# Storing the last two token tiles by half tiles, one request for both row groups

## The chip, the cores and the metric

The kernel runs on one core of a Trainium2 chip. The metric is the device time of one execution in microseconds. Before the change the median of three runs is 279.37 us (279.22 to 279.82). The profiled execution spans 277.0 us. TensorE's granted clock is full over the whole span.

## The reference

A linear attention with cosine weights feeds a dense layer with a gated activation. With B = 8, H = 8, S = 576, D = 64, d_model = 512 and d_ff = 2048:

```python
q_p, k_p = phi(q, c, s), phi(k, c, s)        # relu(x)*cos and relu(x)*sin, concatenated
kv  = einsum('bhsf,bhsd->bhfd', k_p, v)
num = einsum('bhsf,bhfd->bhsd', q_p, kv)
den = einsum('bhsf,bhf->bhs', q_p, k_p.sum(axis=2)) + 1e-6
x   = (num / den).transpose(0, 2, 1, 3).reshape(4608, 512)
h   = x @ w_in                               # 4608 x 2048
out = (h / (1 + exp(-beta * h))) @ w_out     # 4608 x 512, float32
```

The 4608 token rows are worked on in nine chunks of 512 rows. A chunk has four tiles of 128 rows. Only the last matmul of the last chunk, and the way its result leaves for DRAM, is touched by the change.

## The kernel before

The product with `w_out` is done for a pair of token tiles at once, in seven block products instead of eight (`"1"` to `"7"`), with sums of the operands prepared ahead and sums of the results made while they leave PSUM. `o1` and `o2` are the two 128 x 512 output tiles of the pair in SBUF. Each is written in two halves of 256 columns (HM = 256, DM = 512):

```python
def c4():
    h = HM // 2 if last else HM
    nc.scalar.copy(o2[:, 0:h], b_ps[:, 0:h])
    if last:
        nc.vector.tensor_copy(o2[:, h:HM], b_ps[:, h:HM])
        store(c, pr + 2, o2, 0, HM)

def stored(key, op):
    def do():
        op()
        waits[key[0]].discard(key[1:])
        if not waits[key[0]] and not (last and key[0] == "2"):
            store(c, pr + (2 if key[0] == "2" else 0), o2 if key[0] == "2" else o1)
        if last and key == "2a7":
            store(c, pr + 2, o2, HM, DM)
    return do

waits = {"1": {"a2", "a3"}, "2": {"a7", "c4"}}
# ...
"c4": stored("2c4", c4),
"a2": stored("1a2", lambda: nc.vector.tensor_tensor(o1[:, 0:HM], a_ps, p1, **add)),
"a3": stored("1a3", lambda: nc.vector.tensor_tensor(o1[:, HM:DM], e_ps, u, **add)),
"a7": stored("2a7", lambda: nc.vector.tensor_tensor(o2[:, HM:DM], b_ps, p5, **add)),
```

`last` is true for the second pair of the last chunk, which the list of operations calls `y`; the first pair of that chunk is `x`. The list ends, with the operations that only prepare later chunks left out:

```
ox5 ox4 c4x o7y oy3 o2y o3y oy4 c4y
```

So on VectorE the sums of the last pair come in the order a7 (right half of `o2`), a2 (left half of `o1`), a3 (right half of `o1`), and c4 (left half of `o2`) is last of all. In this text they are called a7y, a2y, a3y and c4y.

The rows of a tile lie in DRAM in two groups. Partition p of the first 64 is row 9p + n of a batch of 576 rows, and partition p of the second 64 is row 9p + n + 1. A store sends one request for each group:

```python
out_v = out.rearrange("(b p n) m -> b n p m", b=B, n=NQ)

def store(c, tt, o_sb, m0=0, m1=DM):
    for hf in range(2):
        bb, n = divmod((c * TCH + tt * P) // HP + hf, NQ)
        eng = nc.gpsimd if c < 7 else (nc.sync, nc.scalar)[hf] if c == NTC - 1 and tt % 2 else nc.sync
        eng.dma_start(out=out_v[bb, n][:, m0:m1], in_=o_sb[hf * HP : (hf + 1) * HP, m0:m1])
```

In the last chunk the tiles 0 and 2 (pair `x`) go to SyncE's queue with both groups; the tiles 1 and 3 (pair `y`) go with the first group to SyncE's queue and with the second to ScalarE's.

Of the kernel before, what the change touches and what calls it, by code (L numbers as in the profile page):

```python
# [16 lines left out]
P = 128  # L17
NQ = 9
# [4 lines left out]
def kernel(  # L23
# [14 lines left out]
    nc = tc.nc  # L38

    B, H, S, D = q.shape  # L40
    DM = H * D
# [3 lines left out]
    TCH = 512  # L45
    NTC = B * S // TCH
    TT = TCH // P
    NB = TCH // 64
    HP = P // 2
# [35 lines left out]
    HM = DM // 2  # L85
# [417 lines left out]

    out_v = out.rearrange("(b p n) m -> b n p m", b=B, n=NQ)

    def store(c, tt, o_sb, m0=0, m1=DM):
        for hf in range(2):
            bb, n = divmod((c * TCH + tt * P) // HP + hf, NQ)
            eng = nc.gpsimd if c < 7 else (nc.sync, nc.scalar)[hf] if c == NTC - 1 and tt % 2 else nc.sync
            eng.dma_start(out=out_v[bb, n][:, m0:m1], in_=o_sb[hf * HP : (hf + 1) * HP, m0:m1])  # L510

    def o_mm(c, tt, jts, cols=1):
        o_ps = ps[:, (2, 3, 0, 1)[tt] if c == 0 else 2 + tt // 2]
        for jt in jts:
            w = DM // cols if jt > 0 else DM
            for m0 in range(0, DM, w):
                nc.tensor.matmul(o_ps[:, m0 : m0 + w], lhsT=gs[c, jt // 4][:, jt % 4, tt * P : (tt + 1) * P],  # L517
                                 rhs=wout[:, jt, m0 : m0 + w],
                                 start=(jt == 0), stop=(jt == JT - 1 and m0 == DM - w))
        if jts[-1] < JT - 1:  # L520
            return
        o_sb = osb_pool.tile([P, DM], FP32, name="o_sb", tag="o_sb")
        nc.scalar.copy(o_sb, o_ps)
        store(c, tt, o_sb)
# [7 lines left out]
    def late(c):  # L532
        made[c] = made.get(c, 0) + 1
        return made[c] > 14 - SPLITS.get(c, (0, 0))[1]

    def o_fast(c, pr, banks):

        b_ps, e_ps, a_ps = (ps[:, k_, 0:HM] for k_ in banks)
        tok = slice(pr * P, (pr + 1) * P)
        last = c == NTC - 1 and pr == 1  # L540

        def prod(dst, left, right, start, stop, pieces=False):
            order = (0, 1, 2, 3, 4, 5, 7, 6) if c + 1 >= B else range(JT // 2)
            for i in order:
                w = HM // 2 if i and pieces else HM
                for m in range(0, HM, w):
                    nc.tensor.matmul(dst[:, m : m + w], lhsT=left(i), rhs=right[:, i, m : m + w],  # L547
                                     start=start and i == 0,
                                     stop=stop and i == order[-1], skip_group_check=True)

        def g_part(r, hf):
            def at(i):
                jt = 2 * i + r
                return gs[c, jt // 4][:, jt % 4, hf * (TCH // 2) + pr * P : hf * (TCH // 2) + (pr + 1) * P]
            return at

        def s_part(t):
            return lambda i: t[:, i, tok]

        o1 = osb_pool.tile([P, DM], FP32, name="o_sb", tag="o_sb")  # L560
        o2 = osb_pool.tile([P, DM], FP32, name="o_sb", tag="o_sb")
        p1 = part.tile([P, HM], FP32, name="p1", tag="p1")
        p5 = part.tile([P, HM], FP32, name="p5", tag="p5")
        u = part.tile([P, HM], FP32, name="u", tag="u")

        def c4():
            h = HM // 2 if last else HM
            nc.scalar.copy(o2[:, 0:h], b_ps[:, 0:h])
            if last:
                nc.vector.tensor_copy(o2[:, h:HM], b_ps[:, h:HM])  # L570
                store(c, pr + 2, o2, 0, HM)

        def stored(key, op):
            def do():
                op()
                waits[key[0]].discard(key[1:])
                if not waits[key[0]] and not (last and key[0] == "2"):
                    store(c, pr + (2 if key[0] == "2" else 0), o2 if key[0] == "2" else o1)
                if last and key == "2a7":
                    store(c, pr + 2, o2, HM, DM)  # L580
            return do

        waits = {"1": {"a2", "a3"}, "2": {"a7", "c4"}}
        add = dict(op=ALU.add)
        return {
            "1": lambda: prod(b_ps, g_part(0, 0), B11, True, False, late(c)),
            "5": lambda: prod(e_ps, s_part(S1), T1, True, False, late(c)),
            "6": lambda: prod(b_ps, s_part(S2), T2, False, False, late(c)),
            "2": lambda: prod(a_ps, g_part(1, 0), B21, True, True, late(c)),
            "7": lambda: prod(b_ps, s_part(S3), T3, False, False, late(c)),  # L590
            "3": lambda: prod(e_ps, s_part(S4), B22, False, True, late(c)),
            "4": lambda: prod(b_ps, g_part(1, 1), T4, False, True, late(c)),
            "c1": lambda: nc.scalar.copy(p1, b_ps),
            "c5": lambda: nc.scalar.copy(p5, e_ps),
            "cu": lambda: nc.scalar.copy(u, b_ps),
# [5 lines that stand above are left out]
# [463 lines left out]
```

## Time and profile before

| what | before |
|---|---|
| median of 3 runs | 279.37 us |
| span of the profiled execution | 277.0 us |
| TensorE busy | 269.3 us |
| last matmul starts | 272.44 us |
| last copy out of PSUM ends (VectorE, L570) | 273.57 us |
| last store request starts (SyncE) | 273.97 us |
| stores requested from 268.9 us on | 10 requests, 1.05 MB |

Times within the execution count from the start of the span. The page of a profile gives busy times of each engine, the span in 40 slices, the DMA queues, the chain of work that ended last, and groups of instructions by source line. DMA q1 is the queue of SyncE and q10 the queue of ScalarE; SPq and ACTq are the instruction queues of these two engines, in which a store is one instruction of about half a microsecond. "To landing" is the time from the start of that instruction to the last of the store's completion signals. A share of DMA time is a share of all 16 DMA engines. L510 is the store, L547 the block products, L568 and L570 the two halves of c4, and L597, L598 and L599 are a2, a3 and a7.

### The profile page before, as it was taken

Reading aid. Unit: us, or ns where it says so; the run is one execution under the profiler, and the core shown is the slowest. Engines: PE = TensorE matmul, PEld = TensorE weight load, DVE = VectorE, ACT = ScalarE, POOL = GpSimd, SP = SyncE. Lnnn points to the kernel's source line nnn. Section 1 sums busy time; section 2 is a strip of 40 time slices with the busy share of each in tenths; the row PEclk is TensorE's granted clock in tenths of the full one; section 3 lists DMA queues with packets and bytes.
Section 4 is the critical chain, followed back from the end, with each engine's and each line's share of the span. In section 5 each row is a group of like instructions: output and inputs, shape, how many; then the busy total and the mean of one; then the engine's idle time right before and its main releaser. Section 6 shows DMA issues by size and latency. Waiting matters only on the chain.

```text
span 277.0 us, 8756 instructions
## 1 busy us (share of the span) xinstructions
PE 269.3 (97%) x3615; PEld 193.5 (70%) x3621; DVE 209.0 (75%) x548; ACT 179.9 (65%) x357; POOL 69.8 (25%) x89
## 2 busy tenths in 40 slices
PE   8889999999999999999999999999999999999993
PEld 8454455446875587549854898788768886888783
DVE  5889977696979885358659995798679779559832
ACT  5778857793236667675767586896685179429811
POOL 1444000606281085006420632016400140000000
PEclk9999999999999999999999999999999999999999
DMA  7999999999998999992898289715400640024006
GB/s 250 373 395 380 394 388 307 373 199 393 213 231 298 280 222 265 381 135 43 211 374 216 49 220 273 130 22 107 114 2 12 116 114 4 0 59 96 2 2 149
DMA packets 50584, 53.98 MB, mean 195 GB/s; under 512 B 31201, under 2 KB 31473, under 8 KB 50545
## 3 DMA queue, kind: packets, MB, share of 16 engines
q1 hardware_dynamic: 47584, 45.82, 58.8%
q0 software_dynamic: 2688, 7.34, 9.6%
q8 instruction: 28, 0.46, 0.7%
q10 hardware_dynamic: 272, 0.27, 0.4%
q14 instruction: 12, 0.09, 0.2%
HBM read 36.71 MB, written 9.44 MB: 167 GB/s over the span
## 4 chain that ended last, share of the span: by engine, by line
PE 91%; DMA 3%; DVE 2%; SPq 1%; issue 1%; ACTq 0%; ACT 0%
PE ps L547 33%; PE ps L380 25%; PE ps L468 11%; PE ps L517 8%; PE ps L422 7%; PE ps L293 4%; DMA raw_v<-in_v_dram 3%; PE ps L272 3%; DVE xs L315 1%; SPq L79 1%; PE ps L352 0%; DVE win L115 0%; PE ps L234 0%; DVE rden L308 0%; DVE vb L209 0%
## 5 line engine op out<-in xcount | busy, mean ns | idle before, releaser
L380 PE MATMUL ps<-xt,win 128*128 128x512 bf16 (+1 forms) x327 | 71.1, 375 | 0.1
L388 ACT ACTIVATE g_t<-ps,beta 128x512 bf16<-128x512 f32 x80 | 54.4, 689 | 17.6 <-PE ps L380 16.7
L380 PEld LDWEIGHTS <-win 128*128 128x128 bf16 x327 | 31.4, 98 | 35.2 <-issue 0.4
L547 PEld LDWEIGHTS <-S 128*128 128x128 bf16 x508 | 47.4, 98 | 5.1
L510 POOL DMA_DIRECT2D out_dram<-o_sb x56 | 30.8, 556 | 72.3 <-DVE o_sb L598 32.7
L413 ACT ACTIVATE g_t<-ps,beta 128x512 bf16<-128x512 f32 x64 | 41.2, 696 | 3.4 <-PE ps L422 2.2
L547 PEld LDWEIGHTS <-g_t 128*128 128x128 bf16 x388 | 35.4, 98 | 3.9
L399 DVE TENSOR_TENSOR S<-g_t 128x512 bf16<-128x512 bf16 (+1 forms) x70 | 24.3, 382 | 10.4 <-ACT g_t L388 8.2
L547 PE MATMUL ps<-wout,g_t 128*128 128x256 bf16 (+1 forms) x254 | 30.2, 267 | 0.0
L547 PE MATMUL ps<-wout,S 128*128 128x256 bf16 (+1 forms) x254 | 29.3, 267 | 0.0
L222 POOL TENSOR_TENSOR qs<-qt,tanr 128x1152 bf16<-128x1152 bf16 x8 | 18.9, 2378 | 40.2 <-DVE S L399 17.2
L547 PE MATMUL ps<-T,S 128*128 128x256 bf16 (+1 forms) x254 | 29.0, 267 | 0.0
L217 ACT ACTIVATE vb<-raw_v,sin 128x256 bf16<-128x256 f32 (+1 forms) x57 | 25.5, 502 | 0.5 <-DMA raw_v<-in_v_dram 0.5
L422 PE MATMUL ps<-xt,win 128*128 128x512 bf16 (+1 forms) x111 | 24.0, 350 | 0.0
L315 DVE TENSOR_TENSOR xs<-ps,rden 128x768 bf16<-128x768 f32 (+4 forms) x26 | 22.8, 884 | 0.8
L517 PE MATMUL ps<-wout,g_t 128*128 128x512 bf16 (+1 forms) x117 | 21.6, 330 | 0.4 <-issue 0.2
L219 DVE TENSOR_SCALAR vb<-raw_v,cos 128x256 bf16<-128x256 f32 x63 | 20.5, 383 | 0.0
L468 PE MATMUL ps<-w_stage 128*128 128x256 bf16 x120 | 20.3, 273 | 0.0
L468 PEld LDWEIGHTS <-w_stage 128*128 128x128 bf16 x160 | 15.5, 98 | 3.9
L517 PEld LDWEIGHTS <-g_t 128*128 128x128 bf16 x123 | 11.6, 98 | 7.7
L222 POOL TENSOR_TENSOR w_stage<-qt,tanr 128x1152 bf16<-128x1152 bf16 x4 | 9.5, 2380 | 28.4 <-DVE den L304 15.1
L547 PE MATMUL ps<-T,g_t 128*128 128x256 bf16 (+1 forms) x134 | 15.6, 261 | 0.0
(104 smaller groups left out, 380.4 us busy)
## 6 DMA issues: line engine op xcount, KB each, us to landing
raw_v<-in_v_dram SPq DMA_DIRECT2D x7, 1152.0 KB, 11.0
raw_k<-in_k_dram SPq DMA_DIRECT2D x7, 1152.0 KB, 9.2
raw_q<-in_q_dram SPq DMA_DIRECT2D x7, 1152.0 KB, 8.2
out_dram<-o_sb POOLq DMA_DIRECT2D x56, 128.0 KB, 4.3
w_stage<-in_moe_w_in_dram SPq DMA_DIRECT2D x3, 1024.0 KB, 13.2
w_stage<-in_moe_w_out_dram SPq DMA_DIRECT2D x2, 1024.0 KB, 7.6
w_stage<-in_moe_w_out_dram SPq DMA_DIRECT2D x4, 512.0 KB, 12.2
out_dram<-o_sb SPq DMA_DIRECT2D x13, 128.0 KB, 2.4
```

Of the source, the lines that this page charges most:

```text
L217: nc.scalar.activation(o, a, AF.Copy, scale=t[:, n : n + 1])
L222: return eng.tensor_tensor(dst.rearrange("q n (g p) -> q n g p", g=2), src.rearrange("q n (g p) -> q n g p", g=2), tanr[:, n0:n1].unsqueez ...
L315: nc.vector.tensor_tensor(o.rearrange("q j n s d -> q j (n s) d"), nv[:, :, a:z, :, 0:D].rearrange("q j n s d -> q j (n s) d"), rden[:, :, ...
L380: nc.tensor.matmul(ps[:, h_bank(c, jt), i * 64 : (i + w) * 64], lhsT=win[jt // 4][:, mi, (jt % 4) * P : (jt % 4 + 1) * P], rhs=xt[:, i : i ...
L388: nc.scalar.activation(gs[c, jt // 4][:, jt % 4], ps[:, h_bank(c, jt)], AF.Silu, scale=beta[:, jt : jt + 1])
L399: return nc.vector.tensor_tensor(o, l, r, op=op)
L413: nc.scalar.activation(gs[c, jt // 4][:, jt % 4], ps[:, bank], AF.Silu, scale=beta[:, jt : jt + 1])
L422: nc.tensor.matmul(ps[:, bank, o * 64 : z * 64], lhsT=win[jt // 4][:, mi, (jt % 4) * P : (jt % 4 + 1) * P], rhs=xt[:, o:z, jp, g * HP : (g ...
L468: nc.tensor.matmul(dst, lhsT=left[:, g], rhs=right[:, :, g * HP : (g + 1) * HP], start=start and g == 0, stop=stop and g == 1, skip_group_ ...
L510: eng.dma_start(out=out_v[bb, n][:, m0:m1], in_=o_sb[hf * HP : (hf + 1) * HP, m0:m1])
L517: nc.tensor.matmul(o_ps[:, m0 : m0 + w], lhsT=gs[c, jt // 4][:, jt % 4, tt * P : (tt + 1) * P], rhs=wout[:, jt, m0 : m0 + w], start=(jt == ...
L547: nc.tensor.matmul(dst[:, m : m + w], lhsT=left(i), rhs=right[:, i, m : m + w], start=start and i == 0, stop=stop and i == order[-1], skip ...
```

## The change

Three things change, all in the last pair of the last chunk. The second row group and the first now go out with one request, for each half tile that a sum of VectorE ends (a7y, a2y, a3y): a7y and a2y on ScalarE's queue, a3y on SyncE's. The tile `o1` is no longer stored whole after its second half; each half is stored when it is summed. And c4y is copied by ScalarE alone, in one copy of 256 columns, where ScalarE and VectorE copied 128 columns each; its store stays as it was, two requests of 64 rows. The aim is to let each half leave as early as it can, with fewer requests in front of the last one, and to have no hand-over between two engines in the last copy.

```diff
+    def store_both(tt, o_sb, m0, m1, eng):
+        bb, n = divmod(((NTC - 1) * TCH + tt * P) // HP, NQ)
+        eng.dma_start(out=out_v[bb, n : n + 2, :, m0:m1], in_=o_sb[:, m0:m1])
+
     def store(c, tt, o_sb, m0=0, m1=DM):
 ...
         def c4():
-            h = HM // 2 if last else HM
-            nc.scalar.copy(o2[:, 0:h], b_ps[:, 0:h])
+            nc.scalar.copy(o2[:, 0:HM], b_ps)
             if last:
-                nc.vector.tensor_copy(o2[:, h:HM], b_ps[:, h:HM])
                 store(c, pr + 2, o2, 0, HM)
 
         def stored(key, op):
             def do():
                 op()
                 waits[key[0]].discard(key[1:])
-                if not waits[key[0]] and not (last and key[0] == "2"):
+                if last:
+                    if key[1] == "a":
+                        tile_, m0 = (o2, HM) if key == "2a7" else (o1, HM if key == "1a3" else 0)
+                        store_both(pr + (2 if key == "2a7" else 0), tile_, m0, m0 + HM,
+                                   nc.sync if key == "1a3" else nc.scalar)
+                elif not waits[key[0]]:
                     store(c, pr + (2 if key[0] == "2" else 0), o2 if key[0] == "2" else o1)
-                if last and key == "2a7":
-                    store(c, pr + 2, o2, HM, DM)
             return do
```

In the program as built, nothing else differs. TensorE and GpSimd have the same instructions with the same waits. VectorE has one copy less. In the last pair SyncE has two requests (a3y, c4y) where it had three, and ScalarE still has three (a7y, a2y, c4y). A `store_both` request has the pattern [2 rows apart by 512][64 rows apart by 4608][256 columns] on its DRAM side, counted in elements, and [128 partitions][256 columns] on its SBUF side. A `store` request has [64][256 or 512] on both sides.

## The prediction

> **What bounds the kernel now.** I read the page first: the line of busy times and the engine shares of the chain that ended last.
>
> ```profile
> span 277.0 us, 8756 instructions
> ...
> PE 269.3 (97%) x3615; PEld 193.5 (70%) x3621; DVE 209.0 (75%) x548; ACT 179.9 (65%) x357; POOL 69.8 (25%) x89
> ...
> PE 91%; DMA 3%; DVE 2%; SPq 1%; issue 1%; ACTq 0%; ACT 0%
> ```
>
> TensorE is busy 97% of the span and is 91% of the chain. The change touches none of its instructions, so everything up to the last matmul should stay where it is. What can move is what follows: the last matmul starts at 272.44 and the span ends at 277.0, so some 4.3 us are at stake on the good side, 1.5% of the time. On the bad side there is no such limit.
>
> Second, the chain of waits in the window 266 to 277 (start, length, what).
>
> ```profile
> 265.95 5.91 PE ps L547 x54
> ...
> 271.88 0.44 DVE o_sb L598
> ...
> 272.34 0.47 ACTq L510
> ...
> 272.98 0.27 ACT o_sb L568
> ...
> 273.28 0.29 DVE o_sb L570
> ```
>
> The reader should see that the chain leaves TensorE at a3y (L598) and goes through ScalarE's request for the tile that a3y completes (0.47 us in ScalarE's queue), before ScalarE's part of c4y may start at 272.98. VectorE's part waits for ScalarE's (273.28) and ends at 273.57. TensorE's last completion signal in the trace is at 272.73, and the other copies of this line start 0.02 us after theirs, so c4y is about 0.23 us late behind that request.
>
> Third, the timeline of the two queues in the window 268.5 to 278, and the DMA issues in the window 266 to 277 (requests, KB each, median us to landing).
>
> ```profile
> 268.91 5.61 SPq L510 DMA_DIRECT2D out_dram<-o_sb  x7
> ...
> 271.01 1.80 ACTq L510 DMA_DIRECT2D out_dram<-o_sb  x2
> ...
> 273.60 0.47 ACTq L510 DMA_DIRECT2D out_dram<-o_sb  x1
> ```
>
> ```profile
> out_dram<-o_sb SPq DMA_DIRECT2D x5, 128.0 KB, 2.4
> out_dram<-o_sb ACTq DMA_DIRECT2D x2, 64.0 KB, 2.2
> out_dram<-o_sb ACTq DMA_DIRECT2D x1, 128.0 KB, 2.7
> out_dram<-o_sb SPq DMA_DIRECT2D x2, 64.0 KB, 2.4
> ```
>
> Narrower windows give the seven starts of SyncE: 268.91, 269.43, 271.40, 271.92, 272.61, 273.25, 273.97. From 271.40 on it is a queue without a gap: a3y's data are there at 272.31 and its first row group is asked for at 273.25; c4y's are there at 273.57 and are asked for at 273.97. That last request lands 2.1 us later, at 276.07, and 0.93 us of closing barriers follow.
>
> Fourth, the table of stretches (columns: us, busy and count of PE, PEld, DVE, ACT, POOL; then clock, DMA share, GB/s).
>
> ```profile
> 272.00:274.00 2.00, 0.72 (x7) 0.39 (x4) 0.60 (x2) 0.27 (x1) 0.00 (x0) 1.00 0.79 182
> 274.00:275.00 1.00, 0.00 (x0) 0.00 (x0) 0.00 (x0) 0.00 (x0) 0.00 (x0) 1.00 1.03 254
> 275.00:276.00 1.00, 0.00 (x0) 0.00 (x0) 0.00 (x0) 0.00 (x0) 0.00 (x0) 1.00 0.59 168
> ```
>
> The second number from the right is what matters: from 272 to 275 all sixteen DMA engines are nearly full. The tail of this kernel is moved by sixteen engines together, and there is little slack if a part of them drops out.
>
> **What the Trainium skill says.** "DMA: Bandwidth & Descriptors", section "Why a DMA increments its semaphore by 16 and not by 1", says how many engines carry a request from SyncE or ScalarE: take the slowest dimension that is not 1 on each side, and the number is the largest k up to 16 that divides both; and the k engines are the lowest-numbered ones. Its section "Rules for kernel authors" warns that an outermost dimension below 16 confines the whole request to that many engines. The trace before agrees as far as it can: every store has 64 on both sides, and in the window 275.1 to 276 ScalarE's last request shows as 80 packets, which is 64 rows and 16 completion writes, one for each engine. No request of the kernel before has a small outermost dimension, so its trace doesn't test the rule for small k. The same page, section "Queues, rings and completion order", says that the queues of SyncE and ScalarE run on the same sixteen engines, each in its own order. Also this agrees: in 274 to 275 packets of both queues make the share of 1.03 together.
>
> **The change, part by part.**
>
> *The copy.* It removes ScalarE's request of 0.47 us between a3y and c4y, as a2y's request now follows a2y (ready at 271.30) and should be issued by about 272.1. The copy can start at 272.73 + 0.02 = 272.75, takes 0.37 (the row of L568 with 256 columns in the timeline), and ends at 273.13 instead of 273.57: 0.44 us earlier. VectorE's 0.29 us copy and the hand-over go.
>
> *The queue of SyncE.* It has one request less. 271.40, 271.92, then a3y at 272.61 (0.55 long), then c4y at about 273.25 instead of 273.97: 0.72 us earlier. ScalarE's own c4y request comes at 273.16 instead of 273.60. Were that all, the last landing would be at 273.25 + 2.1 = 275.35 and the time 279.37 - 0.7 = 278.65 us.
>
> *The new requests.* Here is the step that decides. A `store_both` request has 2 as its outermost dimension in DRAM and 128 in SBUF; the largest k that divides both is 2. By the page each of the three requests is carried by two engines, and all three by the same two, in place of sixteen. Each of the two then writes 64 rows of 1 KB for each request, 192 in all.
>
> What a 1 KB row costs an engine comes from two answers of the trace, each "packets, MB, share of 16 engines":
>
> ```profile
> q10 hardware_dynamic: 80, 0.07, 22.4%
> q1 hardware_dynamic: 444, 0.88, 100.2%
> ```
>
> The first is the window 275.1 to 276: 0.224 x 16 x 0.9 us = 3.23 us for 64 rows of 1 KB and 16 completions, hence at most 50 ns a row. The second is a window of long loads, 23.5 to 26: 1.002 x 16 x 2.5 us = 40.1 us for 0.88 MB, hence 22 bytes per ns for an engine, and 1 KB = 47 ns, in a stream without pauses. I take 47 ns.
>
> The work of one of the two engines, from its first packet on: three requests, 192 x 0.047 = 9.0 us. Its share of the two whole-group stores of pair `x` (4 rows of 2 KB each): by the window 270 to 270.5, 48 packets took 0.874 x 16 x 0.5 = 7.0 us, 146 ns each, so 8 x 0.146 = 1.2 us. Its share of c4y: 8 x 0.047 = 0.4 us. The sum is 10.6 us. The first packet of a7y appears some 1.2 us after its request at 271.01, at 272.2. The engine is done at 272.2 + 10.6 = 282.8. The completion follows the last packet by about 0.35 us in the trace before (last packets at 275.7, landing at 276.07): 283.15. With the 0.93 us of barriers the span is 284.1, which is 7.1 us more. Were the `x` rows as quick as loads (8 x 0.09) it would be 0.5 us less. I put it at +6.8: 279.37 + 6.8 = **286.2 us**, a ratio of 1.024.
>
> The gains above don't subtract. c4y's rows are appended to rings of the two slow engines, so an earlier copy only waits longer; and a tail of 7 us hides every change of tenths.
>
> **Rivals.**
>
> *The requests spread over sixteen engines after all.* For it: the DRAM side holds 128 rows of equal length, and a generator that counted rows could spread them; the trace before shows no request with a 2 outside. Against it: the page states the rule for exactly this case and says that k = 2 was seen. It would give 278.6 us, 0.3% faster, and the DMA share of the tail would stay near 1 for three microseconds. I give it about 15%.
>
> *The rings fill and ScalarE is stuck.* Two requests on ScalarE's queue put 2 x 65 entries on each of two rings. In the trace before, requests that normally take 0.47 us took 1.4 to 2.8 us in the long loads (at 10.1 and 26.7 to 32.5), where some 115 or more packets per engine were outstanding. So ScalarE may be held in the a2y request by up to 1.5 us and copy c4y late. It would cost nothing as long as the two engines still have work, which they have until about 282. It adds to the time only if the ring runs empty between two requests: up to 1.5 us more, 287.7.
>
> *A row costs more in a long row of writes.* Loads show 47 ns, the last stores of 1 KB up to 50. Stores from 64 partitions with 2 KB rows show 146 ns with all engines at work; half of that for 1 KB is 73 ns and would add 192 x 0.026 = 5 us: 291. With fourteen engines idle I expect less competition, not more, but this keeps the upper side long.
>
> *The two engines share the rows otherwise, or pause at completions.* A few tenths either way.
>
> **Range and chances.** Two engines: 85%. Within that case the lowest sum I can build is 0.046 x 192 + 8 x 0.09 + 0.4 = 9.9 us of work, +6.4 us, 285.8; I allow 2 us below for packets that overlap more than the shares show, and 3.3 above for stalls and slower rows. Range 283.8 to 289.5. The 2% line lies at 284.96, near the low side of this case, so about nine tenths of it is slower by over 2%: 0.77. The rest of it and the sixteen-engine case are within 2%: 0.22. Faster by over 2% would need more than the 4.3 us after the last matmul: 0.01.
>
> **What the changed profile would show.** If I am right: the matmuls end at the same time; c4y's copy is one row of 0.37 us starting near 272.75 or up to 1.5 us later; from 275 to 282 the DMA share is near 2/16 = 0.125 with 40 to 45 GB/s and no engine busy; the three new requests (a7y, a2y, a3y) need about 5, 10 and 9 us to land instead of 2 to 3, as a7y has the engines nearly to itself at first and the other two then share them; and each shows 128 rows with 2 completion packets. If the share of the tail stays above 0.5 and the requests land in 2 to 3 us, the step on k is wrong and so is the prediction. If the share is 0.125 but the tail ends much later, it is the 47 ns. If TensorE's end has moved, I have misjudged the part that I called untouched.

## The result, and the profile after

The median goes from 279.56 us (four runs of the kernel before) to 288.33 us (287.97 to 289.73), a ratio of 1.0324 with a 95% interval of 1.0286 to 1.0362. The kernel after is 3.2% slower. The ratio is taken over all the runs; the quotient of the two medians is 1.0314. The profiled span is 285.8 us where it was 277.0.

The first lines of the page after (span, then busy time, share and instructions of each engine):

```profile
span 285.8 us, 8759 instructions
...
PE 268.5 (94%) x3621; PEld 192.1 (67%) x3621; DVE 208.3 (73%) x547; ACT 180.0 (63%) x357; POOL 69.4 (24%) x89
```

TensorE's busy time is the same within 1 us (it was 269.3), in a span that is 8.8 us longer. All engines have only lost share. The time was added where none of them works. In the trace, TensorE's last completion signal stands at 272.76, and at 272.73 before.

The chain of waits in the window 266 to 286 (start, length, what):

```profile
271.91 0.43 DVE o_sb L603
...
272.35 0.45 ACTq L508
...
272.97 0.37 ACT o_sb L571
```

In this kernel L508 is the new request for both row groups, called the joint request from here on, L514 the plain store, L571 the copy and L603 is a3. The last copy is now one piece of 0.37 us, but it starts at 272.97, no earlier than before: it still stands behind a request in ScalarE's queue, now that of a2y (L508). And the chain ends here, at 273.34, 12.5 us before the span does. It follows instructions, and there are none left; what goes on after that is transfers. Its share of 89% for TensorE on the page would mislead whoever stopped there.

The stretches of the same execution (us, busy and count of PE, PEld, DVE, ACT, POOL; clock, DMA share, GB/s):

```profile
273.00:274.00 1.00, 0.00 (x0) 0.00 (x0) 0.00 (x0) 0.34 (x1) 0.00 (x0) 1.00 0.86 233
274.00:275.00 1.00, 0.00 (x0) 0.00 (x0) 0.00 (x0) 0.00 (x0) 0.00 (x0) 1.00 0.21 43
275.00:276.00 1.00, 0.00 (x0) 0.00 (x0) 0.00 (x0) 0.00 (x0) 0.00 (x0) 1.00 0.37 94
...
278.00:279.00 1.00, 0.00 (x0) 0.00 (x0) 0.00 (x0) 0.00 (x0) 0.00 (x0) 0.50 0.44 84
279.00:280.00 1.00, 0.00 (x0) 0.00 (x0) 0.00 (x0) 0.00 (x0) 0.00 (x0) 0.50 0.13 47
280.00:281.00 1.00, 0.00 (x0) 0.00 (x0) 0.00 (x0) 0.00 (x0) 0.00 (x0) 0.50 0.14 49
...
283.00:284.00 1.00, 0.00 (x0) 0.00 (x0) 0.00 (x0) 0.00 (x0) 0.00 (x0) 0.50 0.07 25
```

Before, the stretch from 274 to 275 had a DMA share of 1.03 and 254 GB/s. Now it falls to 0.21 there. From 275 to 279 it moves between 0.15 and 0.44: in the trace the other fourteen engines carry their part of c4y's two requests at 275 to 276 and at 278 to 279. From 279 to 282 the share sits at 0.13 to 0.14, which is two engines of sixteen, and at the very end at 0.07, which is one. Two engines move 47 to 49 GB/s. The two DMA queues in the window 279 to 281.5 (packets, MB, share of 16 engines):

```profile
q10 hardware_dynamic: 83, 0.08, 9.5%
q1 hardware_dynamic: 35, 0.04, 4.0%
```

All these 118 packets are 1 KB rows, and 0.135 x 16 x 2.5 us = 5.4 us for them is 46 ns a row.

The DMA view of the window 270 to 286 (packets; then the requests issued in it, KB each, median us to landing):

```profile
DMA packets 870, 1.05 MB, mean 66 GB/s; under 512 B 102, under 2 KB 614, under 8 KB 870
...
out_dram<-o_sb SPq DMA_DIRECT2D x4, 128.0 KB, 4.2
out_dram<-o_sb ACTq DMA_DIRECT2D x2, 128.0 KB
out_dram<-o_sb ACTq DMA_DIRECT2D x1, 64.0 KB, 9.3
out_dram<-o_sb SPq DMA_DIRECT2D x1, 64.0 KB, 10.8
```

The two joint requests of ScalarE have no landing time, because the view counts sixteen completion signals for a request, and the trace has only two that come with the data for each joint request. By the later of these two, a7y, a2y and a3y land 5.8, 10.0 and 12.0 us after they were asked for. The two c4y requests of 64 rows, which needed 2.1 and 2.3 us, need 10.8 and 9.3: their share on the two slow engines waits behind the joint rows.

### The profile page after: what moved, and what is told of

The parts are those of the page before. It is cut to its first block, busy times and chain, and to the rows that moved or that the text cites. A ratio compares the mean times of both kernels' runs of the same rounds, so it can differ in the third digit from the quotient of the medians.

```text
span 285.8 us, 8759 instructions
## 1 busy us (share of the span) xinstructions
PE 268.5 (94%) x3621; PEld 192.1 (67%) x3621; DVE 208.3 (73%) x547; ACT 180.0 (63%) x357; POOL 69.4 (24%) x89
## 4 chain that ended last, share of the span: by engine, by line
PE 89%; DMA 3%; DVE 2%; SPq 1%; issue 1%; ACTq 0%; ACT 0%
PE ps L551 32%; PE ps L380 24%; PE ps L468 11%; PE ps L521 7%; PE ps L422 7%; PE ps L293 4%; DMA raw_v<-in_v_dram 3%; PE ps L272 3%; DVE xs L315 1%; SPq L79 1%; PE ps L352 0%; DVE win L115 0%; PE ps L234 0%; DVE rden L308 0%; DVE vb L209 0%
## 5 line engine op out<-in xcount | busy, mean ns | idle before, releaser
L514 POOL DMA_DIRECT2D out_dram<-o_sb x56 | 30.4, 549 | 72.9 <-DVE o_sb L603 32.9
L521 PE MATMUL ps<-wout,g_t 128*128 128x512 bf16 (+1 forms) x123 | 22.3, 333 | 0.0
## 6 DMA issues: line engine op xcount, KB each, us to landing
raw_q<-in_q_dram SPq DMA_DIRECT2D x7, 1152.0 KB, 10.1
```

## The experiments

Where TensorE ends moves by up to 1.4 us between profiled executions of these kernels, although its instructions are the same. So besides the ratio, the table gives the time from TensorE's last completion signal to the last landing, which leaves that out. Each ratio is against runs of the kernel before that were made together with that kernel; their medians are 279.52 to 279.60 us.

| kernel | median us | ratio, 95% interval | TensorE's end to last landing, us |
|---|---|---|---|
| before | 279.56 | 1 | 3.35 |
| after | 288.33 | 1.0324 [1.0286, 1.0362] | 12.09 |
| no joint request | 280.28 | 1.0036 [1.0022, 1.0050] | 3.56 |
| a7y joint | 282.51 | 1.0105 [1.0084, 1.0125] | 5.78 |
| a7y and a2y joint | 285.69 | 1.0216 [1.0199, 1.0233] | 9.37 |
| three joint, a2y by GpSimd | 287.07 | 1.0266 [1.0246, 1.0286] | 10.75 |
| three joint, all by GpSimd | 287.28 | 1.0270 [1.0236, 1.0303] | 8.55 |
| three joint, all by SyncE | 287.93 | 1.0291 [1.0259, 1.0323] | 11.21 |
| before, last request 48 + 16 rows | 279.99 | 1.0015 [0.9998, 1.0031] | 3.50 |
| before, last request 61 + 3 rows | 283.81 | 1.0152 [1.0102, 1.0202] | 6.72 |
| before, copy by ScalarE alone | 279.80 | 1.0009 [0.9988, 1.0030] | 3.35 |
| before, queues shared out anew | 279.87 | 1.0006 [0.9982, 1.0030] | 3.44 |

**No joint request.** Each joint request is sent as two plain ones, and the rest of the change stays: half tiles, their order, the queues and the single copy. The lines are written out here without the branch that the next two runs use.

```diff
-        eng.dma_start(out=out_v[bb, n : n + 2, :, m0:m1], in_=o_sb[:, m0:m1])
+        for hf in range(2):
+            eng.dma_start(out=out_v[bb, n + hf][:, m0:m1], in_=o_sb[hf * HP : (hf + 1) * HP, m0:m1])
```

> The kernel after, with each of its three joint requests sent as two requests of 64 rows on the same queue; half tiles, their order and the copy by ScalarE alone stay. Theory (a joint request runs on two engines because its outermost dimension is 2): all sixteen engines carry the tail again, every request lands in 2 to 3 us, and the last landing is near 276, so 279.4 us, between 278.8 and 280.0. Rival (the half tiles, their order, or the copy by ScalarE alone cost the time): it stays near 288 us. If the 1 KB rows cost 46 ns in place of the 146 ns of 2 KB rows with all engines at work, the packets of the half tiles of o1 show that.

Measured: 280.28 us. Of the 12.09 us after TensorE's end 8.5 are gone. The same DMA view of this kernel:

```profile
DMA packets 960, 1.05 MB, mean 66 GB/s; under 512 B 192, under 2 KB 704, under 8 KB 960
...
out_dram<-o_sb SPq DMA_DIRECT2D x4, 128.0 KB, 2.4
out_dram<-o_sb ACTq DMA_DIRECT2D x5, 64.0 KB, 2.3
out_dram<-o_sb SPq DMA_DIRECT2D x3, 64.0 KB, 2.3
```

The bytes are the same, 1.05 MB, and the packets are 90 more than after. A request of 64 rows brings 16 completion packets. Three joint requests turned into six bring 6 x 16 = 96, and 96 - 90 = 6 is what the three had: two each. With one completion packet for each engine, as the prediction read them, that is the number of engines, counted without any knowledge of rows or times. The kernel was expected at 279.4 and at most 280.0. Its median is 0.7 us over before, of which the longer tail (3.56 instead of 3.35) explains 0.2 us. ScalarE has four requests in front of the last copy here, which starts 0.95 us after TensorE's end (275.12 and 274.16 in the trace). The other 0.5 us is not explained by anything in the tail. By the median its 1 KB rows took 46 ns in ScalarE's queue and 67 in SyncE's.

**One joint request, then two.** The kernel of the first run, with one argument more:

```diff
-        for hf in range(2):
+        if one:
+            eng.dma_start(out=out_v[bb, n : n + 2, :, m0:m1], in_=o_sb[:, m0:m1])
+            return
+        for hf in range(2):
```

with `one` set for a7y alone, and then for a7y and a2y.

> As the run before it, but a7y alone goes out with one joint request. Theory: two engines have 64 rows of 1 KB more, 3.0 us of work, from 272.3 on; with their share of the other requests (2.4 us) they are done at about 277.7 and the last landing is near 278, so 281 to 282 us. Rival (the cost lies in requests that meet each other, not in their rows): one joint request alone costs nothing, 279.4 us.

> As the first run, but a7y and a2y go out with joint requests. Theory: 128 rows for each of the two engines, 6.0 us; done at about 280.5, so 284 to 285.5 us, some 3 us above the run with one joint request and some 3 to 4 us below the kernel after, which has three. Rival: not in proportion to the rows.

Measured: 282.51 and 285.69 us, 0.5 and 0.2 us above the ranges expected. With none and all three, the four tails are 3.56, 5.78, 9.37 and 12.09 us: 2.2, 3.6 and 2.7 us for each joint request, 2.8 on average. 64 rows at 46 ns are 2.9 us. In the same DMA view these two kernels have 930 and 900 packets, 30 fewer for each joint request, which is 32 completions less 2. The cost follows the rows that land on the two engines, and each of the three requests pays it.

**The joint request of a2y by GpSimd.**

```diff
-                                   nc.sync if key == "1a3" else nc.scalar)
+                                   nc.sync if key == "1a3" else nc.gpsimd if key == "1a2" else nc.scalar)
```

> The kernel after, with a2y's joint request issued by GpSimd in place of ScalarE. By the Trainium skill (DMA: Bandwidth & Descriptors, on how many engines a request gets) SyncE and ScalarE always use the lowest-numbered engines, while GpSimd's requests take k consecutive engines from a cursor that moves round. Theory: a2y then runs on another pair, the first pair has 128 rows instead of 192, and the time falls by about 3 us to 284 to 286 us. Rival (all joint requests share one pair, or the cost is in the number of joint requests): it stays within 1 us of 288.

Measured: 287.07 us, 1.3 us below the kernel after. That misses the theory's 284 to 286 and is just inside what the rival allowed. In the trace a3y's rows don't run in earnest before 280.5, when GpSimd's last rows are going through. GpSimd's request moves its rows in packets of 4 KB. From 278.3 to 279.1 the three queues take turns: a 2 KB row of SyncE's queue (84 ns), a 1 KB row of ScalarE's (46 ns) and a 4 KB packet of GpSimd's (159 ns), each starting as the one before it ends, in two such sequences side by side. So GpSimd's request had been given the same two engines, as the rival said. Its 16 packets for each engine are 25 ns shorter than four rows of 46 ns, so an estimated 0.4 us of the 1.3 is the packets' size.

**All three by GpSimd.**

```diff
-                                   nc.sync if key == "1a3" else nc.scalar)
+                                   nc.gpsimd)
```

> The kernel after, with all three joint requests issued by GpSimd. The run with a2y alone on GpSimd fell by 1.3 us only, and its trace let a3y start as the GpSimd rows ended: GpSimd's first request of this kind seems to have used the same two engines. The Trainium skill lets GpSimd's requests take k engines from a cursor that moves on. Theory: the 56 requests before, of 16 engines each, leave the cursor where it was, so a7y takes the first pair, a2y the second, a3y the third; each pair has 64 rows, some 3 us, and the three overlap. GpSimd's requests are slower to start, so 283 to 285 us. Rival (one pair for all): 192 rows on one pair, 287 us or more.

Measured: 287.28 us, a miss by the median. The transfers did what the theory said: the last landing comes 8.55 us after TensorE's end, 3.5 us sooner than in the kernel after, and the three requests overlap. They do start later: the first 4 KB packet comes 2.0 us after the first request, where ScalarE's first joint row came 1.3 us after its own. GpSimd's queue in the window 277.4 to 278.9 (packets, MB, share of 16 engines):

```profile
q0 software_dynamic: 176, 0.13, 33.5%
```

0.13 MB in 1.5 us is 87 GB/s for joint requests alone, where the two engines of the kernel after moved 47 to 49. Packets of 4 KB in 159 ns make 52 GB/s for two engines at most, and the share of 33.5% is 5.4 engines of sixteen. So the three were not all on the same two. It agrees with the Trainium skill, "DMA: Bandwidth & Descriptors", section "Why a DMA increments its semaphore by 16 and not by 1", which gives GpSimd's requests consecutive engines from a cursor that moves on. What the theory left out is the end: after the last landing at 281.70 the span goes on for 3.23 us instead of 0.92 (before) and 0.98 (after). In the trace GpSimd's last drain lasts to 284.16. What it waits for isn't shown.

**All three by SyncE.**

```diff
-                                   nc.sync if key == "1a3" else nc.scalar)
+                                   nc.sync)
```

> The kernel after, with all three joint requests on SyncE's queue, behind the two whole-tile requests of pair x. This is about the 1.5 us by which the two engines finished later than the prediction's sum of work. Theory: those come from single packets of the x tile's rows that took 0.3 to 1.1 us (normally 0.08 to 0.15) where packets of two queues met on the two engines; in one queue they don't meet. The first joint row then starts at about 273.8 instead of 272.3, and 192 rows in 8.9 us end at 282.9: span near 284.3, 286.5 to 287.3 us, below the kernel after in spite of the later start. Rival (the stalls belong to long requests for two engines as such): 289 to 290 us.

Measured: 287.93 us; the median is 0.6 above the theory's range and below the rival's. TensorE happens to end at 273.78 in its profile, 1.0 us later than after. Its joint rows start at 274.87 and the last landing is at 284.99, 10.1 us for the whole of the joint work; after, they are 272.34 and 284.85, 12.5 us. So three requests in one queue, behind the rows of pair x instead of among them, take 2.4 us less. Counted from TensorE's end they start 1.5 us later, so 0.9 us of it is left in the tail and 0.4 us in the median.

This run showed something more. The stretch of SyncE's queue in the timeline, and ScalarE's DMA queue in the window 275 to 278 (packets, MB, share of 16 engines):

```profile
275.91 3.71 SPq L514 DMA_DIRECT2D out_dram<-o_sb  x1
```

```profile
q10 hardware_dynamic: 55, 0.05, 40.6%
```

ScalarE's queue has one request here, c4y's second group, asked for at 274.21. On fourteen engines it has nothing in front of it. Yet 0.406 x 16 x 3 us = 19.5 us for 55 packets is 0.35 us a packet, where a 1 KB row takes 46 ns, and its landings on the fourteen lie between 278.0 and 278.8, some 4 us after the request instead of 2.1 to 2.3. A request for two engines also slows packets on engines it doesn't use. By what, no run here shows.

**Plain requests of 48 and 16 rows, and of 61 and 3.** The kernel before, with the last request of ScalarE cut in two:

```diff
-            eng.dma_start(out=out_v[bb, n][:, m0:m1], in_=o_sb[hf * HP : (hf + 1) * HP, m0:m1])
+            cuts = (0, 61, HP) if hf and (m0, m1) == (0, HM) else (0, HP)      # or 48 in place of 61
+            for r0, r1 in zip(cuts, cuts[1:]):
+                eng.dma_start(out=out_v[bb, n][r0:r1, m0:m1], in_=o_sb[hf * HP + r0 : hf * HP + r1, m0:m1])
```

> The kernel before, with ScalarE's last request (64 rows of c4y) cut into two of 48 and 16 rows; the control for the next run. Both sizes are divided by 16. All theories: one request more in ScalarE's queue, half a microsecond after the other, lands near 276.2: at most 0.3 us more than before, 279.5 to 279.9 us.

> The same cut at 61 and 3 rows, with plain two-dimensional requests on both sides. Theory (the number of engines is the largest up to 16 that divides the slowest dimension): 61 is prime, so one engine has 61 rows of 1 KB, 2.8 us, from about 275.1 on; the last landing comes at about 278.3, 2.2 us after that of the kernel before: 281.5 to 282.3 us. Rival (the joint requests were slow because of their third dimension or their two row groups): as the control, 279.5 to 279.9 us.

Measured: 279.99 and 283.81 us, the latter 1.5 us above the range expected. The same bytes in the same number of requests, and 3.8 us between them. The DMA view of the window 273.9 to 281, first of the kernel with 48 and 16, then of the one with 61 and 3:

```profile
q10 hardware_dynamic: 176, 0.20, 11.9%
...
out_dram<-o_sb ACTq DMA_DIRECT2D x1, 48.0 KB, 2.2
out_dram<-o_sb ACTq DMA_DIRECT2D x1, 16.0 KB, 2.2
```

```profile
q10 hardware_dynamic: 148, 0.20, 12.2%
...
out_dram<-o_sb ACTq DMA_DIRECT2D x1, 61.0 KB
out_dram<-o_sb ACTq DMA_DIRECT2D x1, 3.0 KB
```

ScalarE's queue has 28 packets fewer with the same rows. The requests of 48 and 16 rows bring 16 completion packets each, so those of 61 and 3 rows have 32 - 28 = 4 together: one engine and three, the largest numbers up to 16 that divide 61 and 3. In the trace one signal with data comes for the 61 rows and three for the 3 rows. The stretch from 278 to 279 of the latter kernel:

```profile
278.00:279.00 1.00, 0.00 (x0) 0.00 (x0) 0.00 (x0) 0.00 (x0) 0.00 (x0) 0.50 0.07 25
```

A share of 0.07 and 25 GB/s is one engine, as in the last microsecond of the kernel after. There is neither a third dimension nor a second row group here, so it is the divisor that counts. The loss is larger than the 2.2 us expected: 61 rows at 46 ns are 2.8 us, and the tail is 3.2 us longer than that of 48 and 16. In the trace 2 KB rows of SyncE's queue took 0.5 to 0.6 us each around 275.6, and in the window 275.4 to 275.9 that queue's 20 packets make a share of 117%, 0.47 us a packet. So many at a time are not on the few engines of the cut request alone: the same slowing of neighbours as above.

**The copy by ScalarE alone, on the kernel before.**

```diff
-            h = HM // 2 if last else HM
-            nc.scalar.copy(o2[:, 0:h], b_ps[:, 0:h])
+            nc.scalar.copy(o2[:, 0:HM], b_ps)
             if last:
-                nc.vector.tensor_copy(o2[:, h:HM], b_ps[:, h:HM])
```

> The kernel before, with c4y copied by ScalarE alone; all requests as before. Theory: the copy still waits for ScalarE's request of o1 and ends some 0.2 us earlier (0.37 us in one piece in place of 0.27 and 0.29 in turn), but SyncE's last request starts only when its queue is through, at 1.24 us after TensorE's last completion signal, as before: no change of the last landing, 279.3 to 279.8 us, ratio 0.999 to 1.001. Rival (the hand-over between the two engines set the end): 0.2 us less in the last landing as well.

Measured: 279.80 us, and the tail is 3.35 us to the hundredth. ScalarE's own request starts earlier (0.66 us after TensorE's end instead of 0.87), but SyncE's last one starts at 1.21 against 1.24, after its queue. The hand-over in the last copy cost nothing that the tail shows.

**A try at beating both.** The kernel before with the copy by ScalarE alone, only requests of 64 rows, and the queues shared out anew: ScalarE sends a7y's groups and one of x's o2 before the last copy; SyncE sends both groups of `o1`. `store_row_groups` sends one plain request of 64 rows for each (group, engine) of its list.

```diff
 ...
+                if c == NTC - 1 and pr == 0 and key == "2c4":
+                    store_row_groups(pr + 2, o2, 0, DM, [(0, nc.sync)])
+                    held.append(lambda: store_row_groups(pr + 2, o2, 0, DM, [(1, nc.scalar)]))
+                elif last and key == "1a3":
+                    store_row_groups(pr, o1, 0, DM, [(0, nc.sync), (1, nc.sync)])
 ...
-                    store(c, pr + 2, o2, HM, DM)
+                    store_row_groups(pr + 2, o2, HM, DM, [(1, nc.scalar), (0, nc.scalar)])
+                    held.pop()()
```

> A try at a version that beats both: the kernel before with the copy by ScalarE alone, all requests of 64 rows, and the queues shared out anew: ScalarE sends both groups of a7y and then the second group of o2 of pair x before the last copy, SyncE sends both groups of the whole o1. Theory: the copy is no longer behind the request of o1 (0.1 to 0.2 us), SyncE's last request starts some 0.85 us after TensorE's last completion signal in place of 1.24, and the last landing comes 2.9 us after that signal in place of 3.3: 279.1 us, ratio 0.998 to 0.999. If the sixteen engines were the limit of the tail, not the queues of requests, the last landing stays at 3.3 us.

Measured: 279.87 us, no difference from before. The copy was not earlier, 0.25 us after TensorE's end in both, as ScalarE's third request now stood in front of it. SyncE's last request starts 0.80 us after TensorE's end, as planned, and lands 2.64 us later where it was 2.1, so the tail is 3.44 us. Asking earlier only made the request wait longer for its transfer: with requests on sixteen engines, the engines and not the queues set the last 3.4 us. The share of 1.03 from 274 to 275 in the kernel before had said so; from 272 to 274 it was 0.79, not as full as the prediction's "from 272 to 275" has it.

## Why the prediction was right, and where its size was off

The time measured, 288.33 us, lies in the range of 283.8 to 289.5, slower by over 2% as expected, and 2.1 us above the 286.2 predicted. The mechanism was the one predicted; one term of its sum was too small.

- *TensorE's part is untouched.* Right: 272.76 and 272.73.
- *A joint request runs on two engines.* Right, and shown by the share of 0.13 to 0.14 and by the two completion packets a request. The plain requests of 61 and 3 rows, on one engine and on three, show that the divisor makes it so.
- *All three run on the same two.* Right for SyncE and ScalarE, whose requests add up in the runs with none, one, two and three of them and leave the share at two engines.
- *A 1 KB row costs 47 ns.* Right: at 47 to 49 GB/s for two engines, 1 KB takes 42 to 44 ns, and the packets of the trace 46.
- *The gains don't count.* Right, and less than thought of them was real: the copy started at 272.97, not at 272.75, since a7y's joint request held ScalarE's queue for 1.13 us instead of half a microsecond. The copy alone and the better queues gained nothing even on sixteen engines, where I had put the gain of both together at 0.7 us.
- *The share of pair x's rows, 8 x 0.146 = 1.2 us.* This is the term that was mis-sized. From the first joint row to the last landing I had 10.95 us and it was 12.5. The run with all three on SyncE's queue, where those rows are through before the joint ones start, needed 10.1, against 200 rows x 0.046 + 0.35 = 9.55 of plain work. So the rows of pair x, meeting the joint rows on the two engines from another queue, seem to have cost 2.4 us instead of 1.2; single 2 KB rows took 0.86, 0.91 and 1.06 us in the trace. That run also put the joint requests themselves in one queue, so the 2.4 us are not all shown to be those rows'. The other 0.35 us is joint work that ran with small pauses. Toward the end one of the two engines finished 1.7 us before the other, which is the share of 0.07. Most of what remains of the 2.1 us is small terms: 0.3 us that I took off my own sum, and a first row 0.14 us later.
- *The times to landing, and the share.* Said: 5, 10 and 9 us for a7y, a2y and a3y, and a share near 0.125 from 275 on. Measured: 5.8, 10.0 and 12.0 us, and that share only from 279 on. I had left out that c4y's requests keep the other fourteen engines at work in parts of the time before.
- *The rival that the rings fill.* ScalarE's a2y request took 0.53 us, so ScalarE was not stuck in it. SyncE's c4y request took 2.66 us in its queue, so requests were held up, but after the copy and beside work of the two engines. Whether that alone would cost anything was not tried apart.

The rival that I gave 15%, sixteen engines, is out. The run with no joint request comes nearest to it, with sixteen engines but six requests for three. It is at 280.28 us, so the 0.3% of gain expected there didn't show either.

## What to carry to other kernels

Before joining two stores into one, look at the slowest dimension of both sides as the request carries it, and find the largest number up to 16 that divides both. In the requests of SyncE and ScalarE here, that many engines did the work: two for an outer dimension of 2, one for 61 rows, three for 3, and sixteen for 16, 48 and 64. A short outer dimension, or a number of rows without a large divisor, can turn a saved half microsecond of issue into several microseconds of transfer (2.8 us for each of the three here). At the end of this kernel nothing hid them; elsewhere it was not tried. In a profile it shows as a DMA share near 1/16 or 2/16 with no engine busy, and as requests whose landing isn't counted.

## What was not expected of the hardware

- A request for one or two engines slowed packets on other engines and in the other queue: 0.35 us for a 1 KB row on engines that had nothing else to do, and SyncE's next request took 2.7 to 3.7 us in its queue instead of 0.5. What causes it is open.
- GpSimd's three joint requests overlapped on more than two engines (87 GB/s together), but GpSimd ended 3.2 us after the last landing instead of 0.9.
- In requests of 64 rows, 2 KB rows took about 150 ns in the tail before and 1 KB rows 46. After, many 2 KB rows of the same two requests of pair x came later and took 84. Why 2 KB cost more than twice 1 KB was not tried.
